# A written-out order of the attention's tasks in place of a planner, scores of two query tiles in one run, and a last key block of whole rows

## The chip, the cores and the metric

One core of a Trainium2 chip runs the whole program. The metric is device time in microseconds (us), taken over several executions; one further execution is recorded by the hardware profiler. Durations below are from that recorded execution. TensorE is PE (its weight loads PEld), VectorE is DVE, ScalarE is ACT, GpSimd is POOL, and SyncE, which issues most DMAs, is SP.

## The reference

An attention with a compressive memory feeds a mixture of experts with one expert per token. B, H, S, D = 4, 8, 576, 64; 2304 tokens of width 512; 8 experts of width 1024; all in float32.

```python
scores = scale * q @ k.T ; scores = where(causal, -1e9, scores)
a = exp(scores - max) / (sum + 1e-9)
local = a @ v
q_p = where(q > 0, q, exp(q) - 1) + 1
mem_out = (q_p @ M_prev) / (q_p @ z_prev + 1e-6)
x = sigmoid(beta) * mem_out + (1 - sigmoid(beta)) * local
e_idx = argmax(x @ w_gate)            # one expert per token
out = gate * eom * (relu(x @ w1[e]) @ w2[e])
```

## The kernel before

**The attention.** Two heads of one batch stand one above the other in the 128 partitions: 16 pairs, numbered g = 0 to 15, four to a batch. In a pair the 576 queries are five query tiles, four of 128 rows and one of 64 rows; for query tile qt only the keys up to its own block are used. Each step is a task with a name that the document uses:

- `load`, `load_v` fetch q and k, and v. `C` casts q and k to their high part, `R` subtracts to get the low part `lo` (POOL). `F0`, `F1`, `F2` make the memory's feature map `phi` (POOL, ACT, DVE).
- `SS{g}_{qt}` makes the scores of one query tile for both heads, as three products of high and low parts. For qt 0 to 3 each head has 64 rows of the array, so two matmuls stand above each other, in tiles of 64 x 128 (line 533); for qt 4 the two heads are stacked in one full tile (line 525).
- `M` takes the maximum on DVE (tiles `st`, `nm`; line 587), `E` the exponential on ACT (line 592), `T` transposes the result on PE (`pt`, line 604), `V` copies it from PSUM into the tile `PT` on ACT or DVE (line 460).
- `P{g}_{q0}` multiplies `PT` with v (`po`, line 640): each head has 64 columns of the array, in tiles of 128 x 64. The fifth key block has 64 rows only, so its matmuls are in tiles of 64 x 64. `O` copies the result into `oT`.
- Per batch: `ME` (memory product, bank pairs `me`, line 690) with `N1`, `N2`, `G` on DVE; `LT`, `LS`, `LY`, `LB`, `LA` (logits of the gates; `LT` in tiles of 128 x 32); `RT`, `RK`, `T...`, `SEL` (routing: choice of the expert, rank of a token, selection tables `selp`); `PV`, `Y`, `XD`, `OUT` (the tokens' rows to DRAM). For the last batch `PL`, `YL`, `TL`, `XL`, `OL` take the place of the latter.

All other matmuls fill the whole 128 x 128 array.

**PSUM.** Of its eight banks the scores have three (`pss`), the transposes two (`pst`), and everything else three (`psm`: `po`, `me`, `mw`, `pv`, `pl`, `lt`, `ls`, `rk`).

**What sets the order.** Nothing reorders the program after it is built: each engine runs its instructions in the order in which the tasks are emitted. That order comes from `arrange`, which keeps a list of ready tasks, estimates when each could start (engine free, inputs done, buffers released), and takes the earliest; among equals the lower due time. Due times are the step number plus an offset from the table `DUE`. A change of tile shape on PE (`mode`: R for 64 x 128, C for 128 x 64 and 128 x 32, F for full) is counted as `SWITCH = 100` ns of a task's time, after the task has been chosen. Copies out of PSUM may go to ACT or DVE, whichever would end first.

**After the attention** the routing of the last batch runs alone (`route`, `rank`, `tail_rank`), then slots of 128 tokens are gathered by indirect DMA, and the experts run slot by slot, PE being busy throughout.

Of the kernel before, what the change touches and what calls it, by code (L numbers as in the profile page):

```python
# [59 lines left out]

class Task:
    def __init__(self, name, eng, cost, fn, due, after=(), takes=(), uses=(), mode=None, size=0, start=0, port=False):
# [3 lines left out]
        self.size, self.start, self.port = size, start, port  # L66


def arrange(tasks, free, turn):

    by = {t.name: t for t in tasks}
    users = {}
    for t in tasks:
        for u in t.takes + t.uses:
            users.setdefault(u, []).append(t.name)
    done, began, order = {}, {}, []
    free, mode = dict(free), [None]
    taken = {u for us in turn.values() for u in us}
    sent = free.pop("DMA")
    left = {t.name: len(t.after) for t in tasks}  # L80
    nexts = {}
    for t in tasks:
        for a in t.after:
            nexts.setdefault(a, []).append(t.name)
    ready = [t.name for t in tasks if not left[t.name]]

    def released(tag, extra):
        old = turn.get(tag, [])
        n = len(old) + extra - BUFS.get(tag, 1)
        if n < 0:  # L90
            return 0
        if n >= len(old):
            return None
        us = users[old[n]]
        if any(u not in done for u in us):
            return None
        return max(done[u] for u in us)

    base = {}

    def earliest(t):
        at = base.get(t.name)
        if at is None:
            at = base[t.name] = max([t.start] + [done[a] for a in t.after])
        if any(u not in taken and u not in t.takes for u in t.uses):
            return None
        extra = {}
        for tag, _ in t.takes:
            r = released(tag, extra.get(tag, 0))
            if r is None:  # L110
                return None
            extra[tag] = extra.get(tag, 0) + 1
            at = max(at, r)
        return at

    while ready:
        best = None
        for eng in free:
            cands = []
            for n in ready:  # L120
                t = by[n]
                if eng in t.cost:
                    at = earliest(t)
                    if at is not None:
                        at = max(at, free[eng], free["POOL"] if t.port and eng == "DVE" else 0)
                        if len(t.cost) > 1:
                            ends = {e: max(at, free[e]) + c for e, c in t.cost.items()}
                            if min(ends, key=ends.get) != eng:
                                continue
                        cands.append((at, t.due, n))  # L130
            if cands:
                first = min(c[0] for c in cands)
                at, due, n = min((c for c in cands if c[0] <= first + LOOK), key=lambda c: (c[1], c[0]))
                if best is None or at < best[0]:
                    best = at, n, eng
        assert best, [n for n in ready]
        at, n, eng = best
        t = by[n]
        cost = t.cost[eng]
        if eng == "PE":  # L140
            if t.mode != mode[0]:
                cost += SWITCH
            mode[0] = t.mode
        began[n] = at
        free[eng] = at + cost
        done[n] = at + cost + AFTER[eng]
        if t.port and eng == "DVE":
            free["POOL"] = max(free["POOL"], at + cost)
        if t.size:
            sent = done[n] = max(sent, at + SEND) + RATE * t.size  # L150
        taken.update(t.takes)
        for u in t.takes:
            turn.setdefault(u[0], []).append(u)
        ready.remove(n)
        order.append((t, eng))
        for x in nexts.get(n, ()):
            left[x] -= 1
            if not left[x]:
                ready.append(x)
    assert len(order) == len(tasks), [n for n, k in left.items() if k and n not in done][:9]  # L160
    return order, began, done
# [7 lines left out]
def attn_moe(ctx: ExitStack, tc: tile.TileContext, qk, vd, mz, mt, rz, beta, wgo, w1, w2, out):  # L169
# [294 lines left out]
    def pair(g):  # L464
# [36 lines left out]
        if g < NG - 1:  # L501
            value(g, 0, 256, [0, 1], [(0, 2, 630)], due("VA0", k0), due("VA0", k0) + 0.3)
            value(g, 256, 576, [2, 3, 4], [(0, 2, 1050), (2, NQ, 1030)], due("VA1", k0), due("VA1", k0) + 0.3)
        else:
            for k, qt in enumerate(tiles, k0):
                value(g, qt * P, qt * P + ROWS[qt], [qt], [(0, NQ, 600 if qt == 4 else (qt + 1) * 210)], k + 1.5, k + 1.6)

    def step(g, qt, k, have):
# [8 lines left out]
        def score():  # L517
# [10 lines left out]
            lc = slice(TQ + qt * P, TQ + qt * P + P)  # L528
            ss.extend(pss.tile([P, 512], F32, name=f"s{n}_{j}", tag="s")[:, :w] for j in range(2))
            for a, (l, m) in enumerate(terms):  # L530
                for j in range(2):
                    r = slice(64 * j, 64 * j + 64)
                    T.matmul(ss[j], l[r, lc], m[r, KC:KC + w], start=(a == 0), stop=(a == 2))  # L533
# [82 lines left out]
    def probs(g):  # L616
        if "PT" not in pr[g]:
            pr[g]["PT"] = wk.tile([P, 2, NQ, S], F32, name=f"PT{g}", tag="PT", bufs=2)
# [672 lines left out]
```

## Time and profile before

| what | value |
|---|---|
| median of 3 runs | 544.98 us (544.73 to 545.97) |
| the profiled execution | 545.58 us; its span 543.8 us |
| PE busy over the span | 519.7 us (96%) |
| DVE busy | 341.4 us (63%) |
| ACT busy | 287.5 us (53%) |
| POOL busy | 288.1 us (53%) |

The span is from the first instruction to the last; the execution's own time is 1.8 us longer. A busy PE is not a PE at its peak: matmuls overlap, and their ends are modelled, so what one costs is read from the start of one to the start of the next. The attention runs from the start to about 228 us, the handoff to about 246 us, the experts from there on.

### The profile page before, as it was taken

To read this page: it belongs to the slowest core of one execution; us is meant where nothing else is said; L and a number is where in the kernel's file an instruction comes from. 1 tells how busy PE (TensorE), PEld (TensorE's weight loads), DVE (VectorE), ACT (ScalarE), POOL (GpSimd) and SP (SyncE) were. 2 spreads that over 40 slices of the span, in tenths; PEclk is the share of its full clock that TensorE was granted. 3 is DMA by queue.
4 is the path that set the end of the run, shared out by engine and by line. 5 is a ranking of instruction groups with operands and counts; after the bars stand their busy time and mean duration, and the time that the engine had idled before them with its cause. 6 is when DMAs were issued, how large, how long until landed. Compare 5 with 4: busy or idle time off the path is not lost.

```text
span 543.8 us, 10539 instructions
## 1 busy us (share of the span) xinstructions
PE 519.7 (96%) x3232; PEld 400.2 (74%) x3232; DVE 341.4 (63%) x806; ACT 287.5 (53%) x658; POOL 288.1 (53%) x262
## 2 busy tenths in 40 slices
PE   8999998999999999849999999999999999999994
PEld 3767766776777677528788888888888888888884
DVE  5697887688878987767989738900052893016510
ACT  4689786878787676136333443333443334433331
POOL 8663375338554441652567646744456566446342
PEclk8699999999999999988999999999999999999999
DMA  7333245225411450139777636831133675115000
GB/s 256 125 131 121 66 127 199 74 68 160 124 28 61 127 128 2 48 100 343 215 215 233 201 121 195 243 124 40 40 108 125 185 217 175 59 40 157 6 4 26
DMA packets 29080, 68.23 MB, mean 125 GB/s; under 512 B 6176, under 2 KB 6688, under 8 KB 29026
## 3 DMA queue, kind: packets, MB, share of 16 engines
q1 hardware_dynamic: 25186, 56.63, 33.9%
q0 software_dynamic: 3696, 10.77, 5.9%
q8 instruction: 32, 0.52, 0.4%
q14 instruction: 22, 0.18, 0.1%
q10 hardware_dynamic: 144, 0.13, 0.1%
HBM read 58.06 MB, written 10.76 MB: 127 GB/s over the span
## 4 chain that ended last, share of the span: by engine, by line
PE 84%; DVE 7%; POOL 3%; issue 3%; ACT 1%; POOLq 0%; DVEq 0%; ACTq 0%
PE h L1106 22%; PE py L1106 21%; PE po L640 9%; PE s L533 7%; PE pt L604 7%; PE me L690 4%; PE hp L1129 3%; PE sd L525 3%; DVE wlo L967 2%; PE px L1075 2%; PE pt L573 2%; PE pv L753 1%; DVE phi L488 1%; PE mw L656 1%; PE lt L782 1%
## 5 line engine op out<-in xcount | busy, mean ns | idle before, releaser
L964 DVE CAST whi<-raw 128x1024 fp32r<-128x1024 f32 x56 | 56.0, 1000 | 119.2 <-ACTq L1113 109.3
L1134 POOL TENSOR_TENSOR hl<-hT,hh 128x512 fp32r<-128x512 f32 x46 | 69.1, 1524 | 87.7 <-ACT hh L1133 87.7
L967 DVE TENSOR_TENSOR wlo<-raw,whi 128x1024 fp32r<-128x1024 f32 x63 | 95.0, 1508 | 3.9 <-ACT whi L964 1.0
L1106 PE MATMUL py<-whi,hh 128*128 (+1 forms) x192 | 77.9, 405 | 1.2 <-DVEq L970 1.2
L592 ACT ACTIVATE st<-st,nm 128x128 f32<-128x128 f32 (+3 forms) x128 | 71.3, 559 | 12.6 <-DVE nm L587 12.0
L1106 PE MATMUL py<-wlo,hh 128*128 (+1 forms) x192 | 74.2, 386 | 0.0
L1106 PE MATMUL h<-whi,xh 128*128 (+1 forms) x184 | 73.9, 402 | 0.0
L1106 PE MATMUL py<-whi,hl 128*128 (+1 forms) x192 | 73.9, 385 | 0.0
L433 POOL TENSOR_TENSOR lo<-qk,hi 128x1216 fp32r<-128x1216 f32 x15 | 41.9, 2793 | 59.0 <-issue 40.1
L1106 PE MATMUL h<-wlo,xh 128*128 (+1 forms) x184 | 73.0, 397 | 0.0
L1106 PE MATMUL h<-whi,xl 128*128 (+1 forms) x184 | 72.5, 394 | 0.0
L587 DVE CUSTOM_DVE_ANT_0 st<-s,mask 128x128 f32<-128x128 f32 (+3 forms) x128 | 59.3, 486 | 19.7 <-PE s L533 11.4
L1119 ACT ACTIVATE h<-h 128x1024 f32<-128x1024 f32 x23 | 23.6, 1027 | 73.3 <-PE h L1106 73.3
L460 ACT COPY PT<-pt 128x512 f32<-128x512 f32 (+2 forms) x94 | 48.0, 526 | 18.0 <-PE pt L604 13.7
L640 PE MATMUL po<-PT,v 128*64 128x320 f32 (+5 forms) x480 | 57.0, 361 | 0.1
L1133 ACT CAST hh<-hp 128x512 fp32r<-128x512 f32 x46 | 27.5, 597 | 48.1 <-PE py L1106 48.1
L604 PE MATMUL pt<-ident,st 128*128 128x128 f32 x320 | 50.0, 287 | 0.7 <-ACT st L592 0.4
L1132 ACT COPY hT<-hp 128x512 f32<-128x512 f32 x46 | 27.2, 591 | 42.7 <-PE hp L1129 38.8
L1083 POOL TENSOR_TENSOR xl<-x,xh 128x512 fp32r<-128x512 f32 x22 | 32.2, 1462 | 33.2 <-ACT x L1082 29.8
L640 PEld LDWEIGHTS po<-PT,v 128*64 128x64 f32 (+1 forms) x480 | 28.0, 137 | 24.2 <-issue 9.4
L604 PEld LDWEIGHTS pt<-ident,st 128*128 128x128 f32 x320 | 36.6, 145 | 9.2 <-ACT st L592 5.0
L1106 PEld LDWEIGHTS py<-whi,hh 128*128 128x128 f32 x192 | 36.2, 188 | 7.9 <-DVEq L970 1.9
(196 smaller groups left out, 994.9 us busy)
## 6 DMA issues: line engine op xcount, KB each, us to landing
raw<-in_w SPq DMA_DIRECT2D x64, 512.0 KB, 4.1
qk<-in_qk SPq DMA_DIRECT2D x15, 640.0 KB, 5.7
v<-in_vd SPq DMA_DIRECT2D x16, 320.0 KB, 3.3
xs<-xd SPq DMA_DIRECT2D x12, 256.0 KB, 4.6
mz<-in_mz SPq DMA_DIRECT2D x4, 324.0 KB, 4.1
mt<-in_mt SPq DMA_DIRECT2D x4, 256.0 KB, 3.7
xs<-xa SPq DMA_DIRECT2D x4, 256.0 KB, 4.0
xs<-xd SPq DMA_DIRECT2D x3, 128.0 KB, 2.9
```

Of the source, the lines that this page charges most:

```text
L433: G.tensor_tensor(c["lo"][:, TQ:], c["raw"][:, TQ:], f32(c["hi"])[:, TQ:], op=ALU.subtract)
L460: (A.copy if e == "ACT" else V.tensor_copy)(dst(), src())
L533: T.matmul(ss[j], l[r, lc], m[r, KC:KC + w], start=(a == 0), stop=(a == 2))
L587: V.tensor_tensor_reduce(st[:, :w], ss[j], mask[:, 512 - w:512], -SCALE, 3.0e38, ALU.add, ALU.min, negm()[:, i:i + 1])
L592: A.activation(st, st, AF.Exp, bias=c()["negm"][:, i:i + 1], scale=-1.0, accum_out=sums()[:, qt, 2 * p + j:2 * p + j + 1])
L604: T.transpose(pt[:, (m * k1 + i) * P:(m * k1 + i + 1) * P], st[:, i * P:(i + 1) * P], ident)
L640: T.matmul(po[64 * j:64 * j + 64, qs - q0:q1 - q0], vt[:kk, k, 64 * j:64 * j + 64], PT[:kk, j, k, qs:q1], start=(k == 0), stop=(k == kn - 1))
L964: join((A.copy if eng is A else eng.tensor_copy)(whi[:, e % 2, c, :], raws[e, c]))
L967: join(eng.tensor_tensor(wlo[:, e % 2, c, :], raws.pop((e, c)), f32(whi[:, e % 2, c, :]), op=ALU.subtract))
L1083: G.tensor_tensor(xl, x32, f32(xh), op=ALU.subtract)
L1106: i = T.matmul(o[n % nh], l[:, z], m[:, n * 512 + part.start:n * 512 + part.stop], start=(c == 0 and k == 0 and n < nh), stop=(c == 3 and ...
L1134: G.tensor_tensor(hl[:, z], hT[:, z], f32(hh)[:, z], op=ALU.subtract)
```

## The change

The planner is gone. A text in the source names every task once, in the order in which they are emitted, with the engine of each copy behind a colon; the loop at the end runs down that list. The new list has longer stretches of PE tasks of one tile shape. The table of due times and offsets stays in the file with other numbers, but orders nothing any more.

Beside the order:

- Query tiles 0 and 1 of a pair are scored in one task (`SS{g}_1`): tile 1 in columns 0 to 255 and tile 0 in columns 256 to 383 of the same two banks.
- The scores have four banks in place of three, and `psm` two in place of three.
- `PT` is two fixed tiles, `PT0` and `PT1`, whose rows 64 to 127 of the fifth key block are set to zero once; the value products of that block then use 128 rows, so their tile is 128 x 64 like the others.
- Two `fill` tasks of three small bfloat16 matmuls each stand early in PE's order; their result is not used.
- Several routing steps have one more dependency (`GO`, `CJ`), and the costs of tasks have other numbers, which orders nothing.

```diff
-AFTER = dict(PE=210, ACT=150, DVE=120, POOL=120, SP=0)
-SWITCH = 100
...
+ORDER = """
+first1 load2 SS0_1 M0_0_0 E0_0_0 M0_0_1 M0_1_1 E0_0_1 E0_1_1 first3 first2 M0_1_0 E0_1_0 F00 F01 SS0_3 SS0_2 M0_3_1 load_v2 T0_0 T0_1 M0_3_0 V0_0:DVE
...
+""".split()
...
-BUFS = dict(s=3, pt=2, m=3, st=6, PT=2, qa=2, hi=3, lo=3, v=3, phi=6, mz=2, mt=1, y=2, xd=2, oT=2, lt=1, nm=2, sumd=2, nr=2)
+BUFS = dict(s=4, pt=2, m=2, st=6, PT=2, qa=2, hi=3, lo=3, v=3, phi=6, mz=2, mt=1, y=2, xd=2, oT=2, lt=1, nm=2, sumd=2, nr=2)
...
+    PTS = [wk.tile([P, 2, NQ, S], F32, name=f"PT{i}") for i in range(2)]
...
+            both = [pss.tile([P, 512], F32, name=f"s{n}_{j}", tag="s") for j in range(2)]
+            at = 0
+            for q in (1, 0) if qt == 1 else (qt,):
+                lc = slice(TQ + q * P, TQ + q * P + P)
+                w = (q + 1) * P
+                c()["ss", q] = [x[:, at:at + w] for x in both]
+                at += w
+                for a, (l, m) in enumerate(terms):
+                    for j in range(2):
+                        r = slice(64 * j, 64 * j + 64)
+                        T.matmul(c()["ss", q][j], l[r, lc], m[r, KC:KC + w], start=(a == 0), stop=(a == 2))
...
-                kk = 64 if k == 4 else P
                 for j in range(2):
-                    T.matmul(po[64 * j:64 * j + 64, qs - q0:q1 - q0], vt[:kk, k, 64 * j:64 * j + 64], PT[:kk, j, k, qs:q1], start=(k == 0), stop=(k == kn - 1))
+                    T.matmul(po[64 * j:64 * j + 64, qs - q0:q1 - q0], vt[:, k, 64 * j:64 * j + 64], PT[:, j, k, qs:q1], start=(k == 0), stop=(k == kn - 1))
...
+    for i in range(2):
+        G.memset(PTS[i][64:128, :, 4, 512:576], 0.0)
...
+    def fill(i):
+        w = psm.tile([P, 2, P], F32, name=f"fill{i}", tag="m")
+        for _ in range(3):
+            T.matmul(w, ones, ones.unsqueeze(1).to_broadcast([P, 2, P]), start=True, stop=True)
...
-    order, began, done = arrange(jobs, dict(PE=0, ACT=0, DVE=0, POOL=1500, SP=1500, DMA=7000), held_already)
-    for t, eng in order:
-        t.fn(eng)
+    by = {t.name: t for t in jobs}
+    for item in ORDER:
+        name, _, eng = item.partition(":")
+        by[name].fn(eng)
```

**PE around pair 7, before.** `s7_1_0` is the score tile of pair 7, query tile 1, head 0; `po5_256` the value product of pair 5 for the queries from 256 on; the last number of a name is the buffer's.

```order
L604 MATMUL pt6_3_1_1346<-ident_70,st6_3_1_1306 128x128 x4
L640 MATMUL po6_0_1354<-PT6_1263,v6_1117 64x256 x2
L640 MATMUL po6_0_1354<-PT6_1263,v6_1117 64x128 x2
L533 MATMUL s7_1_0_1367<-lo7_944,hi7_943 128x256
L533 MATMUL s7_1_1_1368<-lo7_944,hi7_943 128x256
L533 MATMUL s7_1_0_1367<-hi7_943,lo7_944 128x256
L533 MATMUL s7_1_1_1368<-hi7_943,lo7_944 128x256
L533 MATMUL s7_1_0_1367<-hi7_943 128x256
L533 MATMUL s7_1_1_1368<-hi7_943 128x256
L640 MATMUL po5_256_1301<-PT5_1121,v5_855 64x320 x2
L640 MATMUL po5_256_1301<-PT5_1121,v5_855 64x192 x2
L640 MATMUL po5_256_1301<-PT5_1121,v5_855 64x64 x2
```

These twelve rows change the tile shape four times (full, 128 x 64, 64 x 128, 128 x 64, 64 x 64).

**PE at the scores of pair 7, now.** Line 497 is the scores' line in the new file.

```order
L497 MATMUL s7_1_0_1335<-hi7_1046 128x256
L497 MATMUL s7_1_1_1336<-hi7_1046 128x256
L497 MATMUL s7_1_0_1335<-lo7_1047,hi7_1046 128x128
L497 MATMUL s7_1_1_1336<-lo7_1047,hi7_1046 128x128
L497 MATMUL s7_1_0_1335<-hi7_1046,lo7_1047 128x128
L497 MATMUL s7_1_1_1336<-hi7_1046,lo7_1047 128x128
L497 MATMUL s7_1_0_1335<-hi7_1046 128x128
L497 MATMUL s7_1_1_1336<-hi7_1046 128x128
L497 MATMUL s7_3_0_1353<-lo7_1047,hi7_1046 128x512
L497 MATMUL s7_3_1_1354<-lo7_1047,hi7_1046 128x512
```

Query tiles 1, 0 and 3 now stand in one run of one shape.

**PE at the value products of pairs 4 and 5, now.** Each `po` tile takes one of the two banks of `psm`.

```order
L607 MATMUL po5_0_1229<-PT1_100,v5_1116 64x256 x2
L607 MATMUL po5_0_1229<-PT1_100,v5_1116 64x128 x2
L607 MATMUL po4_256_1237<-PT0_99,v4_831 64x320 x4
L607 MATMUL po5_256_1256<-PT1_100,v5_1116 64x320 x4
L607 MATMUL po4_256_1237<-PT0_99,v4_831 64x320 x2
L607 MATMUL po4_256_1237<-PT0_99,v4_831 64x192 x2
L607 MATMUL po4_256_1237<-PT0_99,v4_831 64x64 x2
L607 MATMUL po5_256_1256<-PT1_100,v5_1116 64x320 x2
L607 MATMUL po5_256_1256<-PT1_100,v5_1116 64x192 x2
L607 MATMUL po5_256_1256<-PT1_100,v5_1116 64x64 x2
```

Three products that stood apart are one run; `po5_256` takes the bank of `po5_0`, with the four matmuls of `po4_256` between them.

**DVE at the end of the attention, before.** `lg3` holds the last batch's logits; `mx3` is the first step of its routing.

```order
L864 TENSOR_TENSOR yl2_1_3311<-lg3_2832,lgy_3074 128x16
L865 TENSOR_TENSOR yl2_1_3311<-pl2_1_3301,rr3_2755 128x320
L868 TENSOR_REDUCE lg3_2832<-yl2_1_3311 128x16
L267 TENSOR_REDUCE mx3_3338<-lg3_2832 128x5
L271 TENSOR_TENSOR dl3_3340<-lg3_2832,mx3_3338 128x40
```

**DVE at the same place, now.**

```order
L836 TENSOR_REDUCE lg3_2730<-yl2_1_3255 128x16
L280 TENSOR_TENSOR pos2_3268<-rk2_3258,oha_77 128x40
L283 TENSOR_REDUCE ps2_3269<-pos2_3268 128x5
L286 TENSOR_SCALAR ohe_86<-ps2_3269 128x5
L289 TENSOR_TENSOR pcol_76<-ps2_3269,ohe_86 128x5
L811 CAST cntb_83<-cnt_82 128x8
L225 TENSOR_REDUCE mx3_3302<-lg3_2730 128x5
```

Five instructions of the third batch's ranking now stand between the last logits and `mx3`; before they stood further up. On POOL the five `selp` instructions of that batch stand behind the last `XL` now, where before four of them stood between the `XL` instructions.

## Rows read from the trace of the kernel before

**Rows 1.** The page: PE's busy time, its share and instructions; and the granted TensorE clock, in tenths of full speed, in 40 equal slices of 13.6 us.

```profile
PE 519.7 (96%) x3232; PEld 400.2 (74%) x3232; DVE 341.4 (63%) x806; ACT 287.5 (53%) x658; POOL 288.1 (53%) x262
...
PEclk8699999999999999988999999999999999999999
```

**Rows 2.** Busy time in three stretches (attention, handoff, experts): the stretch and its length, then us busy and instructions of PE, PEld, DVE, ACT and POOL, then the granted clock, the DMA share and GB/s.

```profile
0.00:228.40 228.40, 221.38 (x1746) 158.70 (x1747) 180.80 (x635) 167.98 (x461) 119.88 (x140) 0.97 0.36 109
228.40:246.00 17.60, 9.36 (x89) 4.84 (x87) 11.24 (x53) 4.76 (x9) 10.27 (x11) 0.86 0.39 113
246.00:543.80 297.80, 289.01 (x1400) 236.61 (x1400) 149.40 (x122) 114.80 (x189) 157.97 (x112) 0.99 0.44 139
```

**Rows 3.** What PE waited for in the first 230 us, the longest in total: us in total, times, the longest.

```profile
PE s L533 <- DVE nm L587: 2.7, 3, 1.6
```

**Rows 4.** The timeline of PE, 100 to 106 us: start, us from the first start to the last modelled end, then line, operation, tiles, the tile of the array (rows*columns), shape and count. `s` is in tiles of 64*128, `po` of 128*64, the others of 128*128.

```profile
100.66 0.50 PE L533 MATMUL s<-lo,hi 64*128 64x512 f32 x2
100.99 0.40 PE L533 MATMUL s<-hi,lo 64*128 64x512 f32 x2
101.22 0.40 PE L533 MATMUL s<-hi 64*128 64x512 f32 x2
101.55 0.87 PE L604 MATMUL pt<-ident,st 128*128 128x128 f32 x6
102.36 1.30 PE L640 MATMUL po<-PT,v 128*64 128x320 f32 x8
...
104.36 0.30 PE L525 MATMUL sd<-hi 128*128 128x288 f32 x1
104.49 0.82 PE L604 MATMUL pt<-ident,st 128*128 128x128 f32 x6
105.14 1.13 PE L690 MATMUL me<-mz,phi 128*128 128x162 f32 x7
```

**Rows 5.** The costliest groups, shapes kept apart: the value products in tiles of 64*64; count, then us busy and the mean in ns.

```profile
L640 PE MATMUL po<-PT,v 64*64 64x64 f32 x64 | 5.3, 242 | 0.0
```

**Rows 6.** The timeline of all engines, 77 to 86 us, four rows of it; in brackets the idle time before an instruction and what ended it.

```profile
78.81 0.75 DVE L488 SCALAR_TENSOR_TENSOR phi<-qk,phi 128x576 f32<-128x576 f32 x1
...
79.66 2.82 POOL L433 TENSOR_TENSOR lo<-qk,hi 128x1216 fp32r<-128x1216 f32 x1 [2.75 <-ACT hi L429]
...
79.69 3.40 DVE L488 SCALAR_TENSOR_TENSOR phi<-qk,phi 128x576 f32<-128x576 f32 x1
...
84.56 0.78 PE L533 MATMUL s<-lo,hi 64*128 64x384 f32 x2 [1.56 <-DVE nm L587]
```

**Rows 7.** The groups of DVE, shapes kept apart: count, us busy, mean ns; then the idle time before them.

```profile
L488 DVE SCALAR_TENSOR_TENSOR phi<-qk,phi 128x576 f32<-128x576 f32 x16 | 21.3, 1339 | 1.3 <-ACT phi L485 1.3
L703 DVE TENSOR_TENSOR x<-me,nr 128x320 f32<-128x320 f32 x32 | 14.2, 485 | 0.4
L460 DVE COPY PT<-pt 128x512 f32<-128x512 f32 x8 | 5.5, 687 | 1.1 <-PE pt L604 1.0
L696 DVE SCALAR_TENSOR_TENSOR nr<-me,gt 128x4 f32<-128x4 f32 x32 | 4.7, 158 | 4.4 <-PE me L690 4.3
L429 DVE CAST hi<-qk 128x1216 fp32r<-128x1216 f32 x5 | 4.7, 930 | 0.0
L697 DVE RECIPROCAL nr<-nr 128x8 f32<-128x8 f32 x16 | 3.2, 203 | 0.5
L460 DVE COPY PT<-pt 128x384 f32<-128x384 f32 x5 | 2.8, 554 | 0.5 <-PE pt L604 0.5
L460 DVE COPY PT<-pt 128x256 f32<-128x256 f32 x5 | 2.1, 420 | 0.0
L460 DVE COPY oT<-po 128x320 f32<-128x320 f32 x4 | 1.9, 484 | 1.0 <-PE po L640 1.0
L460 DVE COPY lt<-lt 128x288 f32<-128x288 f32 x4 | 1.8, 458 | 1.6 <-PE lt L782 1.6
L460 DVE COPY PT<-pte 64x128 f32<-64x128 f32 x6 | 1.7, 278 | 0.0
L460 DVE COPY oT<-po 128x256 f32<-128x256 f32 x2 | 0.8, 425 | 0.4 <-PE po L640 0.2
```

**Rows 8.** The timeline of all engines around the end of the attention, 214 to 252 us.

```profile
221.90 0.18 DVE L322 TENSOR_TENSOR pos<-rk,oha 128x40 f32<-128x40 f32 x1
222.00 0.15 DVE L843 CAST cntb<-cnt 128x8 bf16<-128x8 f32 x1
...
225.60 3.18 POOL L347 TENSOR_SCALAR selp<-pidx,pcol,tokv 128x128 f16<-128x128 f16 x4
...
229.50 0.68 DVE L864 TENSOR_TENSOR yl<-lg,lgy 128x16 f32<-128x16 f32 x1 [0.66 <-POOL xb L875]
...
230.94 0.20 DVE L267 TENSOR_REDUCE mx<-lg 128x5 f32<-128x40 f32 x1
...
232.78 2.53 PE L204 MATMUL warm<-ones 128*128 128x512 bf16 x11
...
233.29 0.17 DVE L328 TENSOR_SCALAR ohe<-ps 128x5 f32<-128x5 f32 x1
...
235.31 1.17 PE L1000 MATMUL pp<-hit,selp 128*128 128x4 f16 x40
```

More of the change, by code (lines that the diff above doesn't have):

```diff
@@ L61, with __init__ @@
+HOLD = dict(ME=0.0, PV=2.0, LT=1.0)
+EVERY = 2.0
+BUFS = dict(s=4, pt=2, m=2, st=6, PT=2, qa=2, hi=3, lo=3, v=3, phi=6, mz=2, mt=1, y=2, xd=2, oT=2, lt=1, nm=2, sumd=2, nr=2)
 class Task:
-    def __init__(self, name, eng, cost, fn, due, after=(), takes=(), uses=(), mode=None, size=0, start=0, port=False):
+    def __init__(self, name, eng, cost, fn, due, after=(), takes=(), uses=(), mode=None, size=0, start=0, port=False, until=None):
         self.name, self.fn, self.due, self.after = name, fn, due, list(after)
@@ L65, in __init__ @@
         self.takes, self.uses, self.mode = list(takes), list(uses), mode
[L66 to L161, printed above, removed]
@@ L164, in f32 @@
+        self.size, self.start, self.port, self.until = size, start, port, until
 def f32(ap):
@@ L527, in score @@
                 return
[L528 to L533, printed above, removed]
-        job(f"SS{n}", "PE", (330, 360, 530, 700, 800)[qt], due("SS"), score, after=have, takes=[("s", (n, 0)), ("s", (n, 1))], uses=[("hi", g), ("lo", g)], mode="R" if qt < 4 else "F")
+            both = [pss.tile([P, 512], F32, name=f"s{n}_{j}", tag="s") for j in range(2)]
[9 more added lines that the diff above has]
+                        T.matmul(c()["ss", q][j], l[r, lc], m[r, KC:KC + w], start=(a == 0), stop=(a == 2))
+        score_of = n if qt > 1 else f"{g}_1"
+        if qt == 4:
+            job(f"SS{n}", "PE", 790, due("SS"), score, after=have, takes=[("s", (n, 0)), ("s", (n, 1))], uses=[("hi", g), ("lo", g)], mode="F")
+        elif qt:
+            job(f"SS{n}", "PE", (0, 675, 525, 700)[qt], due("SS") - (qt == 1 and g < NG - 1), score, after=have, takes=[("s", (n, 0)), ("s", (n, 1))], uses=[("hi", g), ("lo", g)], mode="R")
         def negm():
@@ L617, in probs @@
         if "PT" not in pr[g]:
[L618 removed]
+            pr[g]["PT"] = PTS[g % 2]
         return pr[g]["PT"]
@@ L708, in memory @@
         gs = range(NP * b, NP * b + NP)
-        job(f"ME{m}", "PE", 1120, due + DUE["ME"], product, after=[f"F2{g}" for g in gs] + [f"MC{b}"] + ([f"Y{b - 1}_{qt}"] if b else []) + held(due + HOLD["ME"]), takes=[("m", (m, 0)), ("m", (m, 1))], uses=[("phi", g) for g in gs] + [("mz", b)], mode="F")
+        job(f"ME{m}", "PE", 1085, due + DUE["ME"], product, after=[f"F2{g}" for g in gs] + [f"MC{b}"] + ([f"Y{b - 1}_{qt}"] if b else []) + held(due + HOLD["ME"]), takes=[("m", (m, 0)), ("m", (m, 1))], uses=[("phi", g) for g in gs] + [("mz", b)], mode="F")
         job(f"N1{m}", "DVE", 460, due + DUE["N1"], norm, after=[f"ME{m}", "gates2"], takes=[("nr", m)], uses=[("m", (m, 0)), ("m", (m, 1))])
@@ L814, in routing @@
         for i, f in enumerate(rs[:5]):
-            job(f"RT{b}_{i}", "DVE", 120, due + DUE["RT"], f, after=[before])
+            job(f"RT{b}_{i}", "DVE", 120, due + DUE["RT"], f, after=[before], port=True)
             before = f"RT{b}_{i}"
@@ L919, in gates2 @@
         G.tensor_scalar(gt, gt, 1.0, 0.0, op0=ALU.add, op1=ALU.add)
+    def fill(i):
+        w = psm.tile([P, 2, P], F32, name=f"fill{i}", tag="m")
+        for _ in range(3):
+            T.matmul(w, ones, ones.unsqueeze(1).to_broadcast([P, 2, P]), start=True, stop=True)
+    for i in range(24):
+        job(f"fill{i}", "PE", 320, 400.0, fill, i, takes=[("m", f"fill{i}")], mode="F", start=6500, until=20000)
     job("first1", "ACT", 400, 0.1, lambda: first(1) and None)
```

94 lines of the change are left out of this document (72 added, 22 removed).

## The prediction, before the changed kernel ran

> **What bounds the kernel now.** I read the page first, then the busy times by stage, then PE's waits, then single rows. PE is busy for 96% of the span [rows 1], so the question is what it is busy with. The stages tell where the change can act: it moves nothing in the experts (297.8 us) and reaches the handoff (17.6 us) only at its entry, so the 228.4 us of the attention are what counts [rows 2]. There PE is busy 221.4 us and idle 7.0; DVE is busy 180.8 and idle 47.6; ACT 168.0; POOL 119.9. PE is the bound, with hardly a wait: the longest in total is 2.7 us in three waits of score matmuls for DVE [rows 3]. The reader is to see next that a busy PE is not all work.
>
> Two groups of six transposes stand 3 us apart [rows 4]. The one at 104.49 lies between matmuls of its own tile shape and takes 0.65 us to the next start (105.14), 0.109 each. The one at 101.55 follows scores in tiles of 64 x 128 and is followed by products in tiles of 128 x 64, and takes 0.81 (to 102.36). So one change of shape into and one out of a group cost 0.16 us. The scores before it show where it lies: their middle pair takes 0.23 us, the first after the change 0.33 and the last before the next change 0.33. Each change thus costs 0.10 us on the last matmul of the old shape and 0.05 (transposes) to 0.10 (scores) on the first of the new one. I take 0.15 us a change, the lower sum, which is also that of the transposes.
>
> **The change part by part.** *Shape changes.* I counted them along PE's instructions from the start to the experts, the 64 x 64 products of the last key block [rows 5] as a shape of their own: 211 before, 92 now. Of the 119 that go, 16 are the steps into 64 x 64 that the padded key block removes; most others fall between scores and transposes or between transposes and value products. 119 x 0.15 = 17.9 us. The number of matmuls and their columns stay the same, the padding included (it adds rows, and each product still streams its 64 columns). The two fill tasks add six matmuls of 256 columns; eleven of 512 columns take 2.53 us [rows 8], so six of half that size cost 0.7. PE's work falls by 17.9 - 0.7 = 17.2 us. One part is in doubt: the 0.05 to 0.10 at the entry might return at each group's first matmul, run or not. Ends: 119 x 0.10 - 0.7 = 11.2 and, with 0.20 a change, 23.1.
>
> [...]
>
> *What DVE does.* The list fixes who copies out of PSUM. DVE's copies: of 512 columns 8 before, 17 now; 384: 5, 9; 256: 5, 2; `oT` of 256: 2, 9; `oT` of 320: 4, 3; `lt`: 4, 2; the small `PT` copy: 6, 7; casts: 5, 4; and one `oT` copy of 64. At the means of [rows 7]: 6.2 + 2.2 - 1.3 + 3.0 - 0.5 - 0.9 + 0.3 - 0.9 + 0.3 (priced as the small copy) = 8.4 us more on DVE, and about as much less on ACT. DVE then has 189.2 us of work in a stage that PE's saving would shorten to 211.2: idle 22.0 in place of 47.6. What hid DVE's delays before is halved, and this is what can take the saving back.
>
> *New waits.* No row shows the new order, so I bound them. Low end: none of the 7.0 us of PE's idle grows, and the 2.7 us behind DVE go as well (below). High end: all 17.2. I take PE's idle time as inversely proportional to DVE's idle time, since the waits shown are for DVE: with x us of new waits, 7.0 x 47.6 / (22.0 + x) = 7.0 + x gives x = 5.2. That is a choice, nearer to the low end because the order leaves work between producer and consumer: counted at the trace's intervals, the median from a query tile's last score matmul to its first transpose is 5.0 us of PE work (6.6 before), and only two tiles of 80 have under 2 us.
>
> *The handoff.* Five small DVE instructions (`pos`, `ps`, `ohe`, `pcol`, `cntb`) now stand ahead of `mx3`, on the path; they take 0.15 to 0.18 each [rows 8], 0.8 together. Against it, the four `selp` that held POOL for 3.2 us at 225.60 no longer stand ahead of the last additions, and DVE waited 0.66 for one of these [rows 8]. The five `selp` now start with `pcol`, just ahead of `mx3`, and with the sixth take 6 x 0.8 = 4.8; before, the first `pp` matmul began 4.4 after `mx3` started, and needs the last `selp` only at its end, so this is hidden to within 0.5. Ends: +0.1 and +1.3; I take +0.8.
>
> *At no cost:* the zeroing of `PT` (two POOL memsets) lies at the start, where POOL also sets up masks; the order of DMAs moves on SP, but `fetch3`, now behind the first store of the last batch, comes some 7 us ahead of `mx3` and its cast runs later still. If that cover were gone, the fourth weight piece would come a few us late. The clock in the first 27 us is 0.8 and 0.6 [rows 1]; a start with other pauses may move its rise by 2 us either way, which is in the range.
>
> *Sum*, against the profiled execution: 545.6 - 17.2 + 5.2 + 0.8 = 534.4 us. The median of the runs is 0.6 below that execution, so 533.8.
>
> **The rivals.** *A, the saving in full.* The longest wait for DVE has a cause that can go: DVE's `phi` update started 0.03 us after a POOL subtraction of 2.82 us and took 3.40 us where it otherwise takes 0.75, and the scores behind it waited 1.56 us [rows 6]. The new list places the sixteen updates afresh; three (`F21`, `F22`, `F215`) stand within ten tasks of a subtraction `R`. If these meetings go and nothing else grows: 545.6 - 17.2 - 2.7 + 0.1 - 0.6 = 525.2. Against it: 22 us of DVE idle for 80 tiles.
>
> *B, the entry is not saved*, as said above: 11.2 us; DVE then idles 28.0, x = 3.5; 545.6 - 11.2 + 3.5 + 0.8 - 0.6 = 538.1.
>
> *C, slower: two banks instead of three for all that is not a score or a transpose.* 123 uses share them. A use must wait until the bank of the use before last is emptied. Counted along the order, the PE work between is under 2 us for 54 uses now (24 before), under 1 us for 19 (one before). Emptying a memory product's bank takes two `nr`, a reciprocal and two `x`: 2 x 0.16 + 0.20 + 2 x 0.49 = 1.5 us on DVE, an `oT` copy 0.48 [rows 7], if DVE is free at once. Where it is not, PE stops. If each of the 54 waits one more copy of 0.48 us, that is 25.9 us: 545.6 - 17.2 + 25.9 + 0.8 - 0.6 = 554.5. It decides from (17.2 - 0.8) / 54 = 0.30 us a use. For it: DVE is nearly full. Against it: no distance is under 0.5 us, and other shapes' work has been put between.
>
> *D, no change: the updates meet POOL more often.* All sixteen at 3.40 us are 54.4 us in place of 21.3 [rows 6, 7]: DVE's work is 189.2 + 33.1 = 222.3, which leaves 6 us of idle time in the old 228.4 and so no room for a gain: 545.0. [...]
>
> That the change doesn't do what it says, fewer shape changes, can't be: PE runs its instructions as listed. That they cost nothing is B carried further.
>
> **How the numbers follow.** The forecast (530 to 538) 0.45; A 0.21; B 0.16; C 0.11; D 0.07. Two times of this kernel closer than 0.2% (1.1 us) cannot be told apart. D is split into 0.04 faster, 0.03 within that; so faster is 0.45 + 0.21 + 0.16 + 0.04 = 0.86, same 0.03, slower 0.11. The range is 525 to 543: it holds the forecast, A and B, and leaves out C, most of D, and a PE price of 0.20 a change with no new wait (522).
>
> **What would show it.** Right: in the first 216 us or so PE has 92 groups by shape, the six-transpose group in one shape still takes 0.65, and the score groups' slow first and last pairs (0.33) are rare; PE's idle time in the attention is about 12 us, and most of its waits name DVE (`nm`, `PT`, `oT`). A: the longest `phi` update stays under 1.5 us and PE idles under 5. B: each group's first pair is slow in the middle of a run too. C: the waits of `me`, `po`, `pv` and `pl` for `x` or `oT` copies add up to over 16 us. D: many `phi` rows near 3 us. I'd be wrong in the working if the attention ended near 215 but the handoff were longer than 17.6 by over 1.3 us, or if the experts, which the change doesn't touch, moved by over 1 us.

## The result and the profile after

The changed kernel takes 526.92 us (median of four runs, 526.39 to 528.30), the kernel before 545.03 on the same chip: a ratio of 0.967, 95% interval [0.964, 0.969]. It is 18.1 us faster. The forecast was 533.8, so its sign was right and 6.9 us of the gain were missed. The profiled execution took 526.39 us.

The page of the changed kernel first, then its three stretches (attention, handoff, experts), with the columns of [rows 2]:

```profile
PE 503.0 (96%) x3238; PEld 402.2 (77%) x3238; DVE 340.9 (65%) x821; ACT 279.1 (53%) x643; POOL 291.1 (56%) x264
...
PEclk9999999999699999889999999999999999999998
```

```profile
0.00:208.00 208.00, 202.01 (x1747) 159.63 (x1748) 180.57 (x647) 159.56 (x446) 119.02 (x140) 0.98 0.38 120
208.00:226.00 18.00, 11.67 (x94) 5.68 (x93) 10.59 (x54) 4.70 (x8) 13.34 (x13) 0.87 0.48 110
226.00:524.40 298.40, 289.30 (x1401) 236.85 (x1400) 149.74 (x122) 114.80 (x190) 158.79 (x112) 0.99 0.44 138
```

Against [rows 2] they give the whole account. The stretches end at round times: from the start of the last `pl` matmul to the first expert matmul, the handoff is 0.7 us longer and not 0.4.

| part of the span | before | now | difference | forecast |
|---|---|---|---|---|
| attention, PE busy | 221.4 | 202.0 | -19.4 | -17.2 |
| attention, PE idle | 7.0 | 6.0 | -1.0 | +5.2 |
| handoff | 17.6 | 18.0 | +0.4 | +0.8 |
| experts | 297.8 | 298.4 | +0.6 | 0 |
| span | 543.8 | 524.4 | -19.4 | -11.2 |

PE's busy time holds the clock too. The page's slow start (PEclk 8 and 6 in [rows 1]) has become full speed, and one slice in mid-attention (the eleventh, 131 to 144 us) has fallen to 6. The stall ahead of it stands in PE's waits of the first 208 us (us in total, times, longest):

```profile
PE pt L572 <- ACT PT L419: 2.4, 1, 2.4
PE warm L162 <- DVE ones L860: 1.1, 1, 1.1
PE s L497 <- POOL lo L404: 1.1, 1, 1.1
PE pt L572 <- ACT st L560: 0.9, 2, 0.6
PE po L607 <- DVE oT L419: 0.4, 1, 0.4
```

The 2.7 us behind `nm` of [rows 3] are gone; one stall of 2.4 us is new. Busy times and the granted clock (the third number from the end) around it:

```profile
118.00:130.30 12.30, 12.30 (x108) 9.47 (x106) 11.22 (x31) 8.70 (x24) 8.42 (x9) 1.00 0.37 107
130.30:132.70 2.40, 0.02 (x2) 0.02 (x1) 2.30 (x10) 1.56 (x5) 0.00 (x0) 0.98 0.64 183
132.70:142.80 10.10, 10.10 (x52) 8.62 (x52) 5.83 (x27) 6.46 (x18) 4.10 (x5) 0.50 0.18 67
```

PE pauses for 2.4 us, and the next 10.1 us run at half clock (granted 0.50): transposes start 0.21 us apart there and `sd` matmuls 0.24, at full clock 0.11 [rows 4] and 0.13. The timeline of DVE and POOL shows who made it wait:

```profile
124.64 1.56 POOL L305 TENSOR_SCALAR selp<-pidx,pcol,tokv 128x128 f16<-128x128 f16 x2
...
125.40 3.58 DVE L229 TENSOR_TENSOR dl<-lg,mx 128x40 f32<-128x40 f32 x1
126.17 2.75 POOL L392 TENSOR_TENSOR lo<-qk,hi 128x1216 fp32r<-128x1216 f32 x1
```

`dl`, a routing step on 40 numbers a row that otherwise takes 0.20 us, ends at 128.98, just behind POOL's subtraction (128.92), and two score maxima queue behind it. Their exponentials on ACT and the copies that PE waits for are late with them. It is the collision of [rows 6] with a small instruction in the place of `phi`; but here DVE's instruction started 0.77 us before the subtraction, while POOL's selections ran.

DVE's groups in the attention, as in [rows 7]:

```profile
L447 DVE SCALAR_TENSOR_TENSOR phi<-qk,phi 128x576 f32<-128x576 f32 x16 | 12.6, 797 | 0.0
L419 DVE COPY PT<-pt 128x512 f32<-128x512 f32 x17 | 11.7, 686 | 1.1 <-PE pt L572 0.5 <-PE pt L541 0.3
...
L229 DVE TENSOR_TENSOR dl<-lg,mx 128x40 f32<-128x40 f32 x3 | 4.0, 1318 | 0.0
```

The copies are there as counted (11.7 against 5.5 us), but the sixteen `phi` updates fell from 21.3 to 12.6 us: the longest now takes 1.52 us, where it was 3.40. `dl` rose to 4.0 from some 1.7.

### The profile page after: what moved, and what is told of

The parts are those of the page before. It is cut to its first block, busy times and chain, and to the rows that moved or that the text cites. A ratio compares the mean times of both kernels' runs of the same rounds, so it can differ in the third digit from the quotient of the medians.

```text
span 524.4 us, 10513 instructions
## 1 busy us (share of the span) xinstructions
PE 503.0 (96%) x3238; PEld 402.2 (77%) x3238; DVE 340.9 (65%) x821; ACT 279.1 (53%) x643; POOL 291.1 (56%) x264
## 4 chain that ended last, share of the span: by engine, by line
PE 84%; DVE 8%; POOL 3%; issue 3%; ACT 1%; POOLq 0%; DVEq 0%; ACTq 0%
PE h L1083 23%; PE py L1083 22%; PE pt L572 7%; PE po L607 7%; PE s L497 6%; PE me L658 4%; PE hp L1106 3%; PE sd L484 2%; DVE wlo L944 2%; PE px L1052 2%; PE pt L541 2%; PE pv L721 1%; POOL selp L305 1%; DVE st L555 1%; PE pl L824 1%
## 5 line engine op out<-in xcount | busy, mean ns | idle before, releaser
L560 ACT ACTIVATE st<-st,nm 128x384 f32<-128x384 f32 (+3 forms) x128 | 71.2, 558 | 14.2 <-DVE nm L555 13.7
L555 DVE CUSTOM_DVE_ANT_0 st<-s,mask 128x128 f32<-128x128 f32 (+3 forms) x128 | 57.9, 483 | 8.4 <-PE s L497 5.3
L392 POOL TENSOR_TENSOR lo<-qk,hi 128x1216 fp32r<-128x1216 f32 x15 | 43.1, 2870 | 27.7 <-ACT hi L388 21.3
L419 ACT COPY PT<-pt 128x512 f32<-128x512 f32 (+2 forms) x84 | 42.1, 516 | 17.9 <-PE pt L572 14.5
L572 PE MATMUL pt<-ident,st 128*128 128x128 f32 x320 | 47.9, 281 | 3.2 <-ACT PT L419 2.4
L1109 ACT COPY hT<-hp 128x512 f32<-128x512 f32 x46 | 27.2, 590 | 42.5 <-PE hp L1106 42.5
L607 PE MATMUL po<-PT,v 128*64 128x320 f32 (+4 forms) x480 | 47.8, 348 | 0.5 <-DVE oT L419 0.4
L607 PEld LDWEIGHTS po<-PT,v 128*64 128x64 f32 x480 | 30.0, 137 | 18.4 <-issue 3.2
```

The lines of the kernel that those rows point to most:

```text
L392: G.tensor_tensor(c["lo"][:, TQ:], c["raw"][:, TQ:], f32(c["hi"])[:, TQ:], op=ALU.subtract)
L419: (A.copy if e == "ACT" else V.tensor_copy)(dst(), src())
L555: V.tensor_tensor_reduce(st[:, :w], c()["ss", qt][j], mask[:, 512 - w:512], -SCALE, 3.0e38, ALU.add, ALU.min, negm()[:, i:i + 1])
L560: A.activation(st, st, AF.Exp, bias=c()["negm"][:, i:i + 1], scale=-1.0, accum_out=sums()[:, qt, 2 * p + j:2 * p + j + 1])
L572: T.transpose(pt[:, (m * k1 + i) * P:(m * k1 + i + 1) * P], st[:, i * P:(i + 1) * P], ident)
L607: T.matmul(po[64 * j:64 * j + 64, qs - q0:q1 - q0], vt[:, k, 64 * j:64 * j + 64], PT[:, j, k, qs:q1], start=(k == 0), stop=(k == kn - 1))
```

## The experiments

Each is timed against the kernel before on the same chip, whose medians there were 546.0 to 546.5; the changed kernel itself was taken again in that series (`e12_same`).

**What a change of tile shape costs.** Two runs, one on each kernel: the padding alone taken out of the changed kernel, and put into the kernel before (with two fixed, zeroed `PT` tiles, the order unchanged).

```diff
+                    kk = 64 if k == 4 else P
-                    ... vt[:, k, ...], PT[:, j, k, qs:q1] ...
+                    ... vt[:kk, k, ...], PT[:kk, j, k, qs:q1] ...
```

> The changed kernel with the 64-row last key block put back in the value product: 21 changes of tile shape more (16 tasks end in such a block; after 5 of them another value product follows, so those cost a change in and one out). Theory S (a change of tile shape costs TensorE 0.15 us, and the fewer changes are the gain): 21 x 0.15 = 3.1 us more than the changed kernel's 526.9, so 530.0; at 0.10 for the exit alone 2.1, so 529.0. Rival O (the gain is in waits, collisions and the clock that the new order has otherwise, a shape change is worth little): under 0.7 us more, so 526.9 to 527.6.

> The kernel before with the last key block padded to 128 rows and nothing else, the order unchanged: in each of 16 tasks the exit of 0.101 us into the 64-row block and its entry of 0.051 go. Theory S: 16 x 0.152 = 2.4 us of TensorE, of which waits may take back a third as in the run without padding: 1.6 to 2.4 less than the kernel before, so 542.6 to 543.4 at 545.0. Rival O (a shape change hardly counts, other waits bound the stage): within 0.7 of before.

Without the padding: 529.64, ratio 0.970 [0.967, 0.973], which is 1.6 to 2.1 us above the changed kernel (0.967 and 0.966 in its two series). Padding the kernel before: 544.35, ratio 0.9969 [0.9949, 0.9989], 1.7 us less. PE's timeline for one value product of pair 1, the changed kernel first and then without the padding:

```profile
34.79 1.20 PE L607 MATMUL po<-PT,v 128*64 128x320 f32 x12
35.92 0.66 PE L541 MATMUL pt<-ident,st 128*128 128x128 f32 x4
```

```profile
35.02 1.34 PE L608 MATMUL po<-PT,v 128*64 128x320 f32 x12
36.29 0.66 PE L541 MATMUL pt<-ident,st 128*128 128x128 f32 x4
```

From the product's start to the next group's: 1.13 and 1.27 us. One step into the 64-row block costs 0.14 to 0.15, with the matmuls one by one 0.10 at the exit and 0.05 at the entry. The 21 steps are 16 into that block and, where another value product follows, five out of it at 0.10 each: 16 x 0.15 + 5 x 0.10 = 2.9 us of PE; the last value product of the attention came only 1.95 us later, since PE's waits shrank (the 2.4 us stall to 2.1, the one of 0.4 for `oT` went). Theory S holds for the price and rival O falls, in the second run by little (its interval just reaches O's 0.7 us). The time rose by less than S's 3.1 us, since a part of the price was paid out of waits. No run prices the changes between scores, transposes and value products one kind at a time; they stand on [rows 4] and on the total below.

**The other parts without the order.** The changed kernel's tasks, arranged by the planner of the kernel before: its code is put back, fills and list are taken out, and the banks are three and three again. The due times and task costs are those that stand in the changed file.

> The changed kernel's tasks (padding and paired scores as they are, no fills, three score banks and three of the others as before) in an order that the planner of the kernel before makes: 186 changes of tile shape in the attention instead of 92. Theory S (0.15 us for each change, nothing else of weight in the order): 94 x 0.15 = 14.1 more than 526.9, so 541, and the last value product ends at about 222 instead of 207.6. Rival O (the order is worth more by the waits and collisions that it avoids): 545 or more, TensorE idle over 10 us in the attention. Rival Q (the shared scores and the padding alone carry the gain): below 535.

555.56, ratio 1.016 [1.012, 1.019]: slower than the kernel before. Its attention as one stretch, with the columns of [rows 2]:

```profile
0.00:240.60 240.60, 225.88 (x1746) 162.24 (x1747) 179.09 (x647) 162.37 (x447) 121.51 (x144) 0.95 0.33 103
```

The longest of PE's waits there:

```profile
PE s L538 <- DVE nm L596: 3.6, 3, 1.8
PE po L648 <- DVE y L766: 3.6, 1, 3.6
```

Rival O's numbers came: PE idles 14.7 us, and its busy time is 23.9 above the changed kernel's. Of these, 96 more changes (188 along its trace) x 0.15 are 14.4, and 6.9 go with the clock, an estimate (240.6 x 0.05 x 2 = 24 us at half against 10.1, and half of the difference); 2.6 are left unexplained. So shared scores and padding bring no gain in this order (rival Q falls), though the padding alone brought 1.7 us in the old one. The list, together with its split of the banks, carries the gain, and about half of what it is worth here lies in waits and clock. The due times were not fitted to these tasks, so this is what the list avoids, not the best that a planner could do.

**The start's clock.** Is the full clock from 8 to 22 us part of the gain, and do the fills hold it? One run leaves the fills out of the list; the other puts six small matmuls behind each of the first two score tasks of the kernel before, where PE pauses.

> The changed kernel without its two fill tasks (six matmuls of ones, about 0.7 us of TensorE). Theory F (the fills keep TensorE at full clock through the first 22 us): half clock returns between about 8 and 22 us as in the kernel before (13.65 us there), up to 6.8 us lost less the 0.7 of the fills, so 530 to 533. Rival P (the closer order alone keeps it, the fills are only work): 526.2 to 527.2 and no half clock before 100 us.

> The kernel before with six small matmuls of ones behind each of the first two score tasks, so that TensorE works through its two pauses of 0.74 and 0.42 us at 6.6 and 8.6 us. Theory C (those pauses drop the clock to half from 8.84 to 22.5 us, and the changed kernel's full clock there is 5 to 6.8 us of its gain): the half clock goes or shrinks to under 4 us, and the time falls by 4 to 6.8 us, 538 to 541. Rival D (the clock drops at the start in some runs whatever these pauses are, or the stage's start waits for casts and loads anyway): half clock still over 8 us, or full clock and less than 2 us gained: 543 to 546.

No fills: 527.39, ratio 0.965 [0.963, 0.967], the same as with them (`e12_same` below: 527.38). Its profile has 3.4 us of half clock from 9.6 us on, but so has the changed kernel's second profile, with the fills, which stand only at 17 us; in its first profile there is none. Theory F (530 to 533) falls: the fills do nothing that can be told from none. The start's clock differs from run to run. The kernel before with warm pauses: 544.96, ratio 0.9975 [0.9956, 0.9994]. Two stretches, 8 to 15 and 15 to 24 us, of the kernel before and then of this run:

```profile
8.00:15.00 7.00, 6.05 (x26) 3.33 (x26) 5.44 (x11) 3.92 (x14) 6.84 (x5) 0.56 0.98 359
15.00:24.00 9.00, 9.00 (x50) 7.58 (x46) 4.92 (x17) 5.25 (x16) 3.91 (x5) 0.58 0.41 139
```

```profile
8.00:15.00 7.00, 4.34 (x30) 2.69 (x31) 5.42 (x11) 3.65 (x12) 6.84 (x5) 0.97 0.94 330
15.00:24.00 9.00, 9.00 (x52) 7.33 (x52) 5.23 (x19) 5.80 (x18) 3.90 (x5) 0.64 0.46 151
```

Half clock fell from 13.7 us (each stretch times its missing clock times two: 7 x 0.44 x 2 + 9 x 0.42 x 2) to 6.9, and the time by 1.4 us only. Between 8 and 15 us PE now idles 2.7 us in place of 1.0: the faster PE waits for its inputs there (DVE and POOL are as busy as before). The time is rival D's. But this run took away only half of the half clock: 6.8 us of it are left from 14.6 us on, where PE is busy throughout, and no run shows what those cost. By the halves it would be 3.4 us, an estimate. So 1.4 of the 18.1 us are shown for the start's clock, and some 3 more are possible.

**The stall in mid-attention.** The late maxima go ahead of `dl`, their exponentials with them; then, in a second run, the cast of the counts too is moved off POOL's next subtraction. Pieces of the list, its line ends left out:

```diff
-M10_3_0 RT1_1 E10_2_1 F113 M10_2_0 E10_3_0 P9_256_0 ... T10_2_1 O9_256:ACT F213 RT1_2 RT1_3 RT1_4 E10_2_0 M10_3_1 RX1 ... SEL0_2 E10_3_1 F215
+M10_3_0 E10_2_1 F113 M10_2_0 E10_3_0 M10_3_1 RT1_1 P9_256_0 ... E10_2_0 ... T10_2_1 E10_3_1 O9_256:ACT F213 RT1_2 RT1_3 RT1_4 RX1 ... SEL0_2 F215
```

```diff
-LB1 load14 CJ0 P8_0_0 ... M11_0_0 CB0 MW3 RK1
+LB1 load14 CJ0 CB0 P8_0_0 ... M11_0_0 MW3 RK1
```

> The changed kernel with the score maxima M10_2_0 and M10_3_1 put ahead of the small DVE subtraction dl of batch 1, which took 3.58 us while POOL worked, and their exponentials moved forward with them. Theory K (that subtraction waits for POOL; the late maxima behind it make TensorE's 2.38 us stall at 130.3, and the stall is what drops the clock to half for 10.24 us after it): stall and half clock go, 2.4 + 5.1 = 7.5 us less than 526.9, so 519.4, and the subtraction is still long. Rival L (the exponentials are late by ScalarE's own queue, or the clock drops anyway at another place): at most 2.4 us less, 524.5 to 526.9, with 10 us of half clock still somewhere.

> The changed kernel with the late dl of e4_late_dl and, besides, the small cast of the counts (cntb of batch 0, which waited 1.38 us for POOL's lo and TensorE for it 1.43) moved 12 us ahead, where POOL's lo isn't running. Theory K (each half-clock stretch begins with a TensorE stall that a small DVE instruction makes by waiting for POOL): the 1.43 us stall and the 3.2 us of half clock behind it go, 1.4 + 1.6 = 3.0 less than e4_late_dl's 522.95, so 520; granted clock full from 24 us to the end of the attention. Rival L (the clock falls at another place, or the next wait takes the time): 522 to 523.

First run: 522.95, ratio 0.958 [0.954, 0.961], some 4.5 us of theory K's 7.5. The stall went from 2.4 to 0.3 us, although `dl` still takes 2.53 us beside the subtraction: what changed is what stands behind it. But 3 us later there is another stall; the timeline of all engines, three rows of it:

```profile
132.00 2.76 POOL L392 TENSOR_TENSOR lo<-qk,hi 128x1216 fp32r<-128x1216 f32 x1 [3.15 <-ACT hi L388]
...
133.41 1.38 DVE L811 CAST cntb<-cnt 128x8 bf16<-128x8 f32 x1
...
134.84 0.18 PE L206 MATMUL rk<-cntb,ones 128*128 128x40 bf16 x1 [1.43 <-DVE cntb L811]
```

A cast of eight numbers a row stood 1.38 us beside POOL's subtraction; PE waited 1.43, and the clock was at half for 3.4 us behind it. In the changed kernel's second profile PE waits for the same cast, too (0.9 us). Second run: 521.28, ratio 0.954 [0.951, 0.956], and the attention ends at 201.2 us with no half clock in it, as the stretch to there shows:

```profile
0.00:201.20 201.20, 195.98 (x1745) 155.67 (x1746) 178.17 (x646) 159.33 (x446) 119.00 (x139) 1.00 0.39 124
```

The cast now takes 0.17 us (at 119.75). The trace is theory K's; the time lies between K's 520 and rival L's 522 to 523, and the two runs' intervals overlap, so the second step's own gain (about 1.7 us) is less sure than the sum of both. The changed kernel thus gave away some 6 us by two small instructions. This version beats both kernels.

**The handoff.**

```diff
-CJ1 P13_256_1 ... T15_4 PLl4_0 M14_2_1 Tgate42 M15_1_0 E14_2_0
+CJ1 CB1 P13_256_1 ... T15_4 RK2 PLl4_0 M14_2_1 Tgate42 M15_1_0 Tpos12 E14_2_0
-XLl1_0 O15_512:DVE ... YLl2_1 RK2 TL3_1 TL2_1 XLl3_1 Tpos12 Tpos22 XLl2_1 Tpos32 Tpos42 SEL2_2 CB2 SEL2_3 SEL2_4 GO2 OL3 SEL2_0 SEL2_1 OL2
+XLl1_0 SEL2_2 SEL2_3 SEL2_4 SEL2_0 SEL2_1 O15_512:DVE ... YLl2_1 TL3_1 TL2_1 XLl3_1 XLl2_1 GO2 OL3 OL2
```

These are pieces of the list again; `CJ2`, `CB2` and the other `Tpos` steps move up between these places.

> The changed kernel with the rank of batch 2, its five small DVE steps and its five POOL selections moved from behind the last value products to about 190 to 202 us, where POOL is idle for 7 us. Theory H (POOL's six selections in a row, about 1.0 us each, hold the row numbers of the first gather back): from the last batch's mx to the first gather 9.1 becomes about 7.6 us, and the mx comes up to 0.8 earlier: 1.5 to 2.3 us less than 526.9, so 524.6 to 525.4. Rival J (the selections meet DVE's work in the attention and delay its last products as much, or the gather waits for something else): 526.6 to 527.5, with the gather at the same place after the last value product.

> e9_early_cb and the moved rank and selections of e5_handoff together. Theory G (after POOL's selections the first gather waits for the write of the last batch's gates, which is sent only when the last rows of xs have landed): the gather stays about 4.8 us behind the issue of that write, whatever POOL does; the time is within 1.0 of e9_early_cb's, 520.3 to 522.3. Rival H (e5_handoff was held back by the extra 0.55 us in its attention alone): 1.0 to 1.5 less, 519.8 to 520.3.

The first run takes 526.48, ratio 0.964 [0.962, 0.966]: no gain that can be told from none, and theory H falls. In the changed kernel `selp` does hold the row numbers back (timeline of all engines):

```profile
209.73 6.01 POOL L305 TENSOR_SCALAR selp<-pidx,pcol,tokv 128x128 f16<-128x128 f16 x6 [0.34 <-DVE pcol L289]
...
215.03 0.35 PE L977 MATMUL pp<-hit,selp 128*128 128x4 f16 x8 [0.73 <-POOL selp L305]
...
216.01 0.16 DVE L982 TENSOR_SCALAR rowi<-pp 128x4 int32<-128x4 f32 x1 [1.55 <-PE pp L977]
```

With them moved, `rowi` comes at 214.46, and still the first gather starts at 218.89 (218.74 before the edit). The write of the last batch's gates and the first gather on the timeline, with the move and then with the move in `e9_early_cb`:

```profile
214.16 0.37 SPq L275 DMA_DIRECT2D xs<-og  x1
...
218.89 1.33 POOL L1033 DMA_INDIRECT xr<-xs,rowi  x1 [5.83 <-issue]
```

```profile
207.63 0.37 SPq L275 DMA_DIRECT2D xs<-og  x1
...
212.24 1.69 POOL L1033 DMA_INDIRECT xr<-xs,rowi  x1 [5.48 <-DVE wlo L944]
```

4.73 and 4.61 us; it was 4.77 in the kernel before (233.79 to 238.56) and 5.99 in the changed one, where `selp` was late. Both moves together: 521.26, the time of `e9_early_cb`, as theory G has it: the gather keeps its distance behind that write. G's reason for the write's own time is not borne out. SyncE's issues with the move, and what the last of them waited for (waits from 200 to 240 us: us in total, times, longest):

```profile
208.72 0.54 SPq L275 DMA_DIRECT2D xs<-og  x1
209.35 1.02 SPq L846 DMA_DIRECT2D xs<-xa  x2
214.16 0.37 SPq L275 DMA_DIRECT2D xs<-og  x1
```

```profile
SPq L275 <- DMA xs<-og: 3.7, 1, 3.7
```

The gates were ready at 212.09. Their write went out 0.05 us after the gates' write of the batch before it had landed (208.72 and 5.4 us), while the last rows of `xs` landed only at 216.5. The same 0.05 us stand in the profiles of the changed kernel (212.70 and 212.75) and of `e11_both` (207.58 and 207.63). In the kernel before, the earlier write was issued at 225.89 and held nothing up. By these times the list, which puts that write (`GO2`) almost last, made this wait; no run moved `GO2` forward, and what that would gain is not shown.

**DVE's load.** Ten copies of transposed weights go from ScalarE to DVE, in the second run ten others from DVE to ScalarE, by the engine behind the colon in the list (`V5_2_1:ACT` to `V5_2_1:DVE`, and so on), both in `e9_early_cb`.

> e9_early_cb with ten copies of transposed weights (groups 5 to 14, 384 or 512 columns each, 0.6 us on DVE) moved from ScalarE to DVE: some 6 us more of DVE work in the attention. Theory W (TensorE's waits grow with DVE's load at the rate that the prediction charged, 5.2 us for 8.4 us of copies, 0.62 per us): 3.7 us more than e9_early_cb's 521.3, so 525, with new TensorE waits that name DVE. Rival V (DVE has that much slack in this order, and TensorE waits only where one instruction is late by a collision with POOL): under 1.0 more, 521 to 522.3.

> The other way round from e10_dve_load: e9_early_cb with ten copies of transposed weights of groups 6 to 12 (about 6 us on DVE) moved from DVE to ScalarE. Theory N (in e9_early_cb TensorE is the bound and DVE stands just under it: more DVE work is paid one for one, less is worth only what idle time is left, 4.1 us of which 2.2 before the second score): at most 1.0 less than e9_early_cb's 521.3, 520.3 to 521.3, or slower where the copies are now late behind ScalarE's exponentials. Rival M (DVE's load sets the stage's length both ways): 4 to 6 us less, 515 to 517.

More on DVE: 527.43, ratio 0.965 [0.963, 0.968], 6 us slower for 6 us of copies. Three new waits of PE and one that has doubled (the last, 0.43 without the move), on its timeline from 88 to 108 us:

```profile
91.08 0.66 PE L572 MATMUL pt<-ident,st 128*128 128x128 f32 x4 [0.57 <-ACT PT L419]
92.39 1.37 PE L658 MATMUL me<-mz,phi 128*128 128x162 f32 x8 [0.65 <-DVE x L671]
95.93 0.63 PE L572 MATMUL pt<-ident,st 128*128 128x128 f32 x4 [0.38 <-DVE PT L419]
106.40 0.87 PE L607 MATMUL po<-PT,v 128*64 128x256 f32 x8 [0.84 <-DVE oT L419]
```

Rival V falls; theory W has the direction and too low a rate. In the profiles PE idles 3.6 us more in the attention (8.8 in place of 5.2); where the rest of the 6 us lies is open. Less on DVE: 524.42, ratio 0.959 [0.956, 0.961], 3 us slower, with four waits (1.6 us) for ScalarE's exponentials in place of two, and in its profile 6.8 us of half clock at the start, where `e9_early_cb` has none. Rival M (515 to 517) falls, and theory N's small gain did not come either; the waits name late exponentials, not the late copies that N allowed for. By the halves that start can be up to 3.4 us, so what the ten copies cost on ScalarE is open. In this order a copy moved to DVE is paid, and one moved away from it brings nothing.

**The changed kernel again.**

> The changed kernel itself again, timed on the same chip as these two, to compare them with it directly: 526.9 at 545.0 for the kernel before, a ratio of 0.967. If the half-clock stretch at 132 us belongs to the order and not to chance, its profile shows the stall of about 2.4 us at 130 and some 10 us of half clock behind it again.

527.38, ratio 0.966 [0.964, 0.968]; the stall is there again (2.4 us at 132.2) and 6.8 us of half clock behind it. It belongs to the order. Over the runs of this kernel the mean clock goes with the time: 526.9 at 0.981, 527.3 and 527.4 at 0.979, 527.9 and 528.8 at 0.976.

## Why the prediction was right, and where its sum was off

- **Shape changes, -17.2.** Right. PE's busy time fell by 19.4. Half clock is 13.7 us before and 10.1 now, worth 1.8 by the halves, an estimate; the fills add 0.6 (0.25 and 0.34 from their start to the next). That leaves 18.2 for 119 changes, 0.153 each, and the padding run shows the two parts, 0.10 and 0.05, by themselves. The count is the right one: the trace shows other short matmuls as 128*64, too (`pte` and parts of `me`, `pv`, `ls`, `pl`), but the step from a transpose to `pte` takes 0.109 us, as within a group. Rival B falls: the padding run shows the entry's 0.05 beside the exit's 0.10, and by this sum 0.153 a change came off, not 0.10.
- **New waits, +5.2.** This step failed. "I take PE's idle time as inversely proportional to DVE's idle time": DVE's idle time came out as the formula had it (27.4 us; 22.0 + 5.2 = 27.2), by luck, since DVE's work and the stage were both over 8 us shorter than reckoned; and with that idle time PE idled 6.0 us, not 12.2. Nor do most of its waits name DVE, as the prediction's sign asked. Over half of the 6.0 is one collision and the wait for the first inputs. A mean over the stage says nothing of whether the next tile is ready. The waits for `nm` are gone (0.2 us at most) wherever the scores have four banks and are there (2.7 to 3.6 us) in all profiles with three; no run has four banks under the old order or three under the new one, so that the fourth bank removed them is not shown alone. That DVE can take the saving back, the reason behind the step, is true in `e9_early_cb`: 6 us more of copies cost 6.
- **DVE's work, 189.2.** Measured 180.6. The copies came as counted; the error is in the terms that were held constant, `phi` first (-8.7).
- **The clock, within 2 us either way.** By the arithmetic -1.8, within the range. The warm start shows 1.4 us for the 6.8 us of half clock where PE waits for inputs anyway. In mid-attention it costs about its half: in `e4_late_dl` it is 6.8 us shorter, PE idles 0.6 less, and the last `pl` matmul starts 3.6 us earlier.
- **The handoff, +0.8.** Measured +0.4 (0.7 by the matmuls), near by luck, since two errors went against each other: the six `selp` took 6.0 us, not 4.8, and were not hidden (1.2 us of PE's waits), and `mx3` came earlier than I counted (2.00 us from the start of the last `pl` matmul, 2.76 before). That the last gates' write would wait for the one before it (0.5 us here) was not foreseen.
- **SP, memsets and experts at no cost.** Experts +0.6, under the 1 us named as a sign of error.
- **Rivals.** A (525.2) came nearest, and its mechanism is what the trace shows: the `phi` updates no longer meet POOL for long and the waits for `nm` are gone. Its two signs were missed by little (the longest `phi` 1.52 us, not under 1.5; PE idle 6.0, not under 5). Its missing 1.7 us are less than what the one new collision costs. C: `po`, `pv`, `pl` and `me` wait 0.4 us in all, not over 16. D: no `phi` near 3 us.

## What to carry to other kernels

A change of tile shape on TensorE costs about 0.15 us here, so count them along the order and price the gain from one pair of timeline groups. Do not turn an engine's mean idle time into waits: look for the single instruction that is late, above all for small DVE instructions beside a long one of GpSimd, since one of them cost 2.4 us of stall and, by half of the 10.1 us at half clock, an estimated 5 more. Before you move a chain off a path, look for the second chain that ends at the same place (here the gates' write behind the row numbers, and behind it an earlier write).

## What was not expected of the hardware

- The size of a DVE instruction did not protect it: 128x40 took 3.58 us and 128x8 1.38 beside a GpSimd subtraction of 2.8 us, 0.20 and 0.17 alone. The cast started 1.41 us behind the subtraction and ended with it (at 134.79 against 134.76), and so did `dl` in `e4_late_dl` (0.30 behind, ended at 128.91 against 128.85). In the changed kernel `dl` started before the subtraction, during a selection, and yet ended with the subtraction (128.98 against 128.92), which had started 0.77 us after it.
- A pause of PE was followed by half clock for very different times: 10.1 us (6.8 in the second profile, `e12_same`) after 2.4 us, 3.4 after 1.4 (`e4_late_dl`), and at the start none after 1.1 (the changed kernel) or 2.2 us (`e9_early_cb`), 3.4 after 1.4 (`e3_nofill`) and 6.8 after 2.2 (`e13_dve_less`).
- The first gather started 4.6 to 4.8 us after the last small write to its source had been issued, in three kernels (4.77 in the kernel before, 4.73 in `e5_handoff`, 4.61 in `e11_both`), and 5.99 in the changed one, where `selp` was late.
